# An early activation-table load, another set of dummy matmuls and a respaced K^TV stage in a two-branch linear-attention kernel

## The chip, the cores and the metric

The kernel runs on one core of a Trainium2 chip. The metric is the device time of one execution in microseconds (us); lower is better. A profile's span is a little over 1 us shorter than the time of the same execution (189.2 against 190.54 us for the kernel before). All comparisons use runs of the fast state only (a kernel has a second, slower state in some executions).

## The reference, cut to what matters

Two linear-attention branches A and B read the same `x` (2048 x 640, bf16). Each has its own weights. A gate mixes them.

```python
g = sigmoid((x * gate_w).sum(-1, keepdims=True))
# each branch: 32 heads of 20 columns
q, k, v = split(x @ wqkv)
phi = lambda t: where(t > 0, t + 1, exp(t)) + 1e-6
pq, pk = phi(q), phi(k)
kv  = einsum("bhsd,bhse->bhde", pk, v)
z   = einsum("bhsd->bhd", pk)
num = einsum("bhqd,bhde->bhqe", pq, kv)
den = einsum("bhqd,bhd->bhq", pq, z) + 1e-6
a   = (num / den) @ wo
out = g * a + (1 - g) * b
```

The kernel never forms `v`. For each branch it makes the keys `phi(K)`, then `G = phi(K)^T x`, from it `K^TV = G Wv` (masked to the heads' blocks), then `W' = K^TV Wo`, and at the end multiplies the scaled queries by `W'`.

## The kernel before

The kernel is written as operations with dependencies; a scheduler at build time gives each engine a fixed order and each result of TensorE one or two banks of PSUM, the memory that TensorE writes to. TensorE follows the order of the program text. The start: dummy matmuls ("warm"), transposes of the first two x tiles on TensorE, then key matmuls of both tiles while weights arrive one 128-row block at a time. In the profile lines XN is x as loaded, XT its transpose, WKW the key weights and `ps` any PSUM bank.

```python
def warm(n):
    for i in range(n):
        op("PE", lambda e: e.matmul(psw(bw, 512), ONE[:, :],
           ONE[:, :].unsqueeze(1).to_broadcast([128, 4, 128]), ...), 430.0, ...)
# ... (cut)
warm(6)
pss = [Buf("k", "ps", 2) for _ in range(2)]
x_tp(0)                          # five transposes of x tile 0
k_step("A", 0, 0, pss[0])        # 512 + 128 columns
x_tp(1)
k_step("A", 0, 1, pss[0])
# ... 18 further key steps of tiles 0 and 1, then for t = 2..15 both branches
```

A finished key tile is turned into phi(K) by ScalarE and VectorE; only then are its PSUM banks free for a later tile:

```python
op("ACT", ... activation(EK[...], psw(ps, D), ACT.Exp) ..., name="ke")       # L533
op("DVE", ... tensor_scalar(EK[...], EK[...], 1.0, EPS, min, add) ..., name="kt")   # L536
op("DVE", ... scalar_tensor_tensor(PKt[X][:, t, :], psw(ps, D), 0.0, EK[...], max, add) ..., name="ks")  # L544
```

Late in the kernel branch B's denominator, K^TV and W' stand between "partial outputs" of branch A (`o_part`, ten matmuls each, which fill TensorE while other engines work):

```python
o_part(0); o_part(1); o_part(2)   # one call per line in the program
den("B")                          # four 32-column matmuls; ScalarE then reads their bank
kv_unit("B")                      # two groups, 20 and 10 matmuls, each into its own bank, then a VectorE mask
o_part(3)
for u in range(NU):               # NU = 6
    wp_unit("B", u)               # two matmuls, then a ScalarE copy
    if u % 2:
        o_part(4 + u // 2)
for t in range(7, NOA):           # NOA = 12 partial outputs in all
    o_part(t)
```

Of the kernel before, what the change touches and what calls it, by code (L numbers as in the profile page):

```python
# [6 lines left out]
ACT = mybir.ActivationFunctionType  # L7
# [67 lines left out]
class Sched:  # L75
# [7 lines left out]
    def op(self, eng, fn, cost, ins=(), outs=(), after=(), prio=None, name="", dma=None):  # L83
        if eng == "ACT" and dma is None:
            after = list(after) + self.consts
        o = Op(eng, fn, cost, list(ins), list(outs), after, len(self.ops) if prio is None else prio, name, dma)
        self.ops.append(o)
        return o
# [171 lines left out]
def body(nc, A_x, A_wqkv, A_wo, B_x, B_wqkv, B_wo, gate_w, out, log=None):  # L260
# [7 lines left out]
    bf, f32 = dt.bfloat16, dt.float32  # L268
    sb = nc.alloc_sbuf_tensor
# [10 lines left out]
    PK = {X: sb("PK" + X, [128, NT * D], bf) for X in XS}  # L280
# [22 lines left out]
    GSf = GS["A"][:, :, :].rearrange("p c f -> p (c f)")  # L303
    PQ["B", 3] = GSf[:, 0:2560].rearrange("p (g s) -> p g s", g=NC)
    FXT = {"A": WV["A"][:, :, :].rearrange("p c f -> p (c f)")[:, 0:2048].rearrange("p (b s) -> p b s", b=NB), "B": XNf[:, 0:2048].rearrange("p (b s) -> p b s", b=NB)}
    NOA = 12
    OA = [XNf[:, 2048 + 1280 * i : 3328 + 1280 * i].bitcast(f32) for i in range(6)]
    OA += [PK["B"][:, 1280 * i : 1280 * i + 1280].bitcast(f32) for i in range(6)]
    NEK, NEQ, NOS = 4, 4, 4
    EK = sb("EK", [128, NEK, D], bf)  # L310
    EQ = EK[:, :, :].rearrange("p k f -> p (k f)")[:, 0 : NEQ * 512].rearrange("p (k f) -> p k f", k=NEQ)
# [12 lines left out]
    GG = sb("GG", [128, 2, NT], f32)  # L324
    GT = sb("GT", [128, 32], f32)
    ONE = sb("ONE", [128, 128], bf)
    EPSC = sb("EPSC", [128, 1], f32)
    PS = nc.alloc_psum_tensor("ps", [128, 8, 512], f32)

# [7 lines left out]
    op = sch.op  # L337

    def psw(b, w):
        return PS[:, b.slot : b.slot + b.n, :].rearrange("p a b -> p (a b)")[:, 0:w]  # L340
# [15 lines left out]
    def mm_cost(n):  # L356
        return n / 2.4 + 2.5

    def act_cost(n):
        return 190 + 0.833 * n  # L360

    def dve1(n):
        return 155 + 1.04 * n
# [5 lines left out]
    bxn = [Buf("xn%d" % t) for t in range(NT)]  # L369
    bxt = [Buf("xt%d" % t) for t in range(NT)]  # L370
    bwk = {(X, c): Buf("wk%s%d" % (X, c)) for X in XS for c in range(NC)}
    bcst, bone, beps, bgwb = Buf("cst"), Buf("one"), Buf("eps"), Buf("gwb")
    bwq = {X: Buf("wq" + X) for X in XS}
    bwv = {X: Buf("wv" + X) for X in XS}
    bwo = {X: Buf("wo" + X) for X in XS}

    op("DVE", lambda e: e.memset(ONE[:, :], 1.0), 120.0, outs=[bone], name="one")
    sch.consts = [op("POOL", lambda e: e.memset(EPSC[:, :], EPS), 100.0, outs=[beps], name="eps")]
    bxo = Buf("xo")
    op("POOL", lambda e: e.memset(XN[:, :, D : D + 1], 1.0), 200.0, outs=[bxo], name="xones")  # L380

# [45 lines left out]

    bw = Buf("warm", "ps")

    def warm(n):  # L430
        for i in range(n):
            op(
                "PE",
                lambda e: e.matmul(psw(bw, 512), ONE[:, :], ONE[:, :].unsqueeze(1).to_broadcast([128, 4, 128]), start=True, stop=True),  # L434
                430.0,
                ins=[bone],
                outs=[bw],
                name="warm",
            )

    def x_tp(t):
        for lo, hi in ((0, 1), (1, 3), (3, 5)):
            bt = Buf("tp", "ps")
            for c in range(lo, hi):
                op(
                    "PE",
                    lambda e, c=c, lo=lo, bt=bt: e.matmul(  # L447
                        PS[:, bt.slot, 128 * (c - lo) : 128 * (c - lo) + 128],
                        XN[:, t, 128 * c : 128 * c + 128],
                        IDN,  # L450
                        start=True,
                        stop=True,
                    ),
                    100.0,
                    ins=[bxn[t], bcst],
                    outs=[bt],
                    name="tp%d" % t,
                )
            half = Buf("xth")
            op(  # L460
                "DVE",
                lambda e, lo=lo, hi=hi, bt=bt: e.tensor_copy(
                    XT[:, lo:hi, 128 * t : 128 * t + 128],
                    PS[:, bt.slot, 0 : 128 * (hi - lo)].rearrange("p (c s) -> p c s", c=hi - lo),
                ),
                dve1(128 * (hi - lo)),
                ins=[bt],
                outs=[half],
                name="tpc%d" % t,
            )  # L470
            bxt[t].parts = getattr(bxt[t], "parts", []) + [half] * (hi - lo)
# [22 lines left out]
    def k_step(X, t, c, ps):  # L494
        w = D + 1 if X == "B" else D

        def fn(e):
            a = psw(ps, w)
            l = XT[:, c, 128 * t : 128 * t + 128]
            e.matmul(a[:, 0:512], l, WK[X][:, c, 0:512], start=(c == 0), stop=(c == NC - 1))  # L500
            return e.matmul(a[:, 512:w], l, WK[X][:, c, 512:w], start=(c == 0), stop=(c == NC - 1))  # L501

        xin = [bxt[t].parts[c] if hasattr(bxt[t], "parts") else bxt[t]]
        op(
            "PE",
            fn,
            mm_cost(512) + mm_cost(128),
            ins=xin + [bwk[X, c]] + ([bgc] if X == "B" else []),
            outs=[ps],
            name="k%s%d_%d" % (X, t, c),  # L510
        )
# [39 lines left out]
    def k_unit(X, t):  # L551
# [2 lines left out]
            k_step(X, t, c, ps)  # L554
        k_post(X, t, ps)

    warm(6)
    pss = [Buf("k", "ps", 2) for _ in range(2)]
    x_tp(0)
    k_step("A", 0, 0, pss[0])  # L560
    x_tp(1)
    k_step("A", 0, 1, pss[0])
    k_step("A", 1, 0, pss[1])
# [13 lines left out]
    for t in range(2, NT):  # L577
# [12 lines left out]
        ins=[bgg, bge2] + bge,  # L590
        outs=[bgg2],
        prio=LOW + 52,
        name="gm",
# [9 lines left out]
    for i, X in enumerate(XS):  # L603
        for j in range(NB):
# [8 lines left out]
                ins=bgd,  # L613
                outs=[b],
# [46 lines left out]
    def kv_unit(X):  # L661
        gv = GS[X][:, :, :].rearrange("p c (g m) -> p c g m", g=NC)
        for us in ((0, 1, 2, 3), (4, 5)):
            ps = Buf("kv", "ps")

            def fn(e, us=us, ps=ps):
                for i, u in enumerate(us):
                    lo = GR * u if u < 5 else D - GR
                    for c in range(NC):
                        r = e.matmul(  # L670
                            PS[0:GR, ps.slot, GR * i : GR * i + GR],
                            WV[X][:, c, lo : lo + GR],
                            gv[:, c, :, lo // 5 : lo // 5 + 24],
                            start=(c == 0),
                            stop=(c == NC - 1),
                        )
                return r

            op("PE", fn, 5 * len(us) * mm_cost(GR), ins=[bwv[X]] + [bgs[X, g] for g in range(NC)], outs=[ps], name="kv" + X)
            b = Buf("kvl")  # L680
            bkvl[X].append(b)
            n = len(us)
            op(
                "DVE",
                lambda e, us=us, ps=ps, n=n: e.tensor_tensor(
                    out=KVL[X][:, us[0] : us[0] + n, :].rearrange("p u (m g) -> p u g m", g=NC),
                    in0=PS[0:GR, ps.slot, 0 : GR * n].rearrange("p (u g m) -> p u g m", u=n, g=NC),
                    in1=BDM.unsqueeze(1).unsqueeze(1).to_broadcast([GR, n, NC, 24]),
                    op=ALU.mult,
                ),  # L690
                dve1(GR * n),
                ins=[ps, bcst],
                outs=[b],
                prio=-1,
                name="kvm",
            )
# [99 lines left out]
    def scale_now(X, b, h):  # L796
        pqs_op[X, b, h].prio = len(sch.ops)
# [32 lines left out]
    def den(X):  # L830
# [17 lines left out]
        for h in range(2):  # L848
# [4 lines left out]
                "ACT",  # L853
                lambda e, q=q: e.activation(DTT[:, q], PS[:, ps.slot, q], ACT.Identity, bias=EPSC[:, 0:1], scale=1.0),
                act_cost(256),
# [86 lines left out]
    def o_part(t):  # L942
        ps, b = Buf("oa", "ps", 2), Buf("oas")
        boa[t] = b
        o_mm("A", t, ps, 0, D, last="A")
        op("ACT", lambda e: e.activation(OA[t], psw(ps, D), ACT.Copy), act_cost(D), ins=[ps], outs=[b], name="oac")

    def o_rest(t):
        ps = Buf("o", "ps", 2)
        o_mm("B", t, ps, 0, D, first="B")  # L950
        o_post(t, ps, 0, D, "ADD")
# [29 lines left out]
    def out_unit(t):  # L981
        ps = Buf("o", "ps", 2)
        for X in XS:
            o_mm(X, t, ps, 0, D)
        o_post(t, ps, 0, D, "ACT")
# [52 lines left out]
    o_part(1)  # L1038
    o_part(2)
    den("B")  # L1040
    kv_unit("B")
    o_part(3)
    for u in range(NU):
        wp_unit("B", u)
        if u % 2:
            o_part(4 + u // 2)
    for t in range(7, NOA):
        o_part(t)
    for b in range(3):
        for h in range(2):  # L1050
            scale_now("B", b, h)
    for t in range(NOA):
        o_rest(t)
    for h in range(2):
        scale_now("B", 3, h)
    for t in range(NOA, NT - 1):
        out_unit(t)
# [41 lines left out]
```

## Time and profile before

| | before |
|---|---|
| time, median of the first 3 runs | 190.91 us (190.69 to 191.21) |
| span of the profile | 189.2 us |
| TensorE busy | 98% |
| first key matmul of the third tile starts | 10.75 us |
| last matmul starts | 186.85 us |

The page's busy table and its chain of waits. In the first line each engine has busy us, its share of the span and its number of instructions; the second gives shares of the span.

```profile
PE 184.9 (98%) x1245; PEld 107.8 (57%) x1269; DVE 127.3 (67%) x251; ACT 95.6 (51%) x171; POOL 0.3 (0%) x6
...
PE 96%; ACT 1%; issue 1%; DVE 1%; DVEq 0%; ACTq 0%
```

TensorE (PE) is both the busiest engine and nearly the whole chain. So a change without fewer matmuls can only close holes between them, or let more of them run at the fast rate (below). The list of waits for TensorE of the kernel before (who waited, for whom, us in total, times, longest) names few:

```profile
PE ps L434 <- DVE ONE L377: 0.4, 1, 0.4
PE ps L500 <- DVE PKA L544: 0.3, 1, 0.3
PE ps L752 <- issue: 0.2, 1, 0.2
```

A recorded matmul lasts longer than the time it blocks the next one: at full rate a 512-column matmul lasts 0.38 us but the next starts 0.216 us after it, a 128-column one 0.22 us and 0.056 us. A hole is therefore best read from start to start. The timeline shows the one in the middle line of the list (start us, us, engine, line, operation, tiles; brackets hold the idle time and its releaser):

```profile
7.48 1.28 ACT L533 ACT_TABLE_LOAD   x1 [7.48 <-PE ps L501]
...
8.77 1.30 ACT L533 ACTIVATE EK<-ps 128x640 bf16<-128x640 f32 x2
...
9.87 0.82 DVE L544 SCALAR_TENSOR_TENSOR PKA<-ps,EK 128x640 bf16<-128x640 f32 x1
...
10.23 0.22 PE L501 MATMUL ps<-WKW,XT 128*128 128x129 bf16 x1
...
10.75 0.39 PE L500 MATMUL ps<-WKW,XT 128*128 128x512 bf16 x1 [0.30 <-DVE PKA L544]
```

The table load stands in front of the first exponential; VectorE ends the tile at 9.87 + 0.82 = 10.69; the third tile's matmul follows at 10.75. From 10.23 it should have started 0.06 us later, so the hole is 0.46 us (0.47 by the unrounded starts).

The start of the same kernel on TensorE:

```profile
0.39 2.74 PE L434 MATMUL ps<-ONE 128*128 128x512 bf16 x6 [0.39 <-DVE ONE L377]
2.93 0.74 PE L447 MATMUL ps<-CST,XN 128*128 128x128 bf16 x5
3.71 0.58 PE L500 MATMUL ps<-WKW,XT 128*128 128x512 bf16 x1
4.09 0.31 PE L501 MATMUL ps<-WKW,XT 128*128 128x128 bf16 x1
4.41 0.45 PE L447 MATMUL ps<-CST,XN 128*128 128x128 bf16 x5
4.83 0.39 PE L500 MATMUL ps<-WKW,XT 128*128 128x512 bf16 x1
```

The key matmul of 512 columns lasts 0.58 us at 3.71 and 0.39 us at 4.83: between them the array goes from a slow to a fast rate. The Trainium skill describes this ("TensorE: Matmul & The Clock Gate", section "Part 1: The HAM clock gate"): a window that runs freely decides it.

The late stage, from the timeline of all engines:

```profile
143.54 0.40 PE L835 MATMUL ps<-TSH,CST 128*32 128x512 bf16 x4
...
143.87 2.02 PE L670 MATMUL ps<-GSB,WVB 128*120 128x120 bf16 x30
...
144.24 0.83 ACT L854 ACTIVATE DTT<-ps,EPSC 128x256 f32<-128x256 f32 x2
...
144.75 0.95 DVE L864 RECIPROCAL RCT<-DTT 128x128 f32<-128x128 f32 x1 [1.44 <-ACT DTT L854]
...
145.62 2.10 DVE L685 TENSOR_TENSOR KVLB<-ps,CST 120x480 bf16<-120x480 f32 x2
...
145.94 1.30 PE L922 MATMUL ps<-WPA,EX 128*128 128x128 bf16 x9
...
147.19 0.40 PE L706 MATMUL ps<-WOB,KVLB 120*120 120x512 bf16 x1
```

The order is denominator (L835), K^TV (L670), a partial output (L922), first W' (L706). A partial output has ten matmuls; the record of its first, of 512 columns, is missing here (x9), as one is about every 7 to 8 us all through this trace (1245 records). I count such a gap as 0.22 us of work.

### The profile page before, as it was taken

The numbers are of one execution on the slowest core, as the hardware profiler recorded it, in microseconds if no ns is written. First come the engines' busy times: TensorE is split into PE (matmuls) and PEld (weight loads), VectorE is DVE, ScalarE is ACT, GpSimd is POOL, SyncE is SP. The second block draws the span as 40 slices with busy tenths as digits, with TensorE's granted clock in tenths as the row PEclk, the third lists the DMA queues.
The fourth block names the chain that finished last, engine by engine and source line by source line (L and its number), as shares of the span: only waits on it lengthen the run. The fifth ranks groups of instructions, "written<-read, shape, count | busy, mean of one in ns | idle before, by whom it ended". The sixth has DMA issues, their size and how long they took to land.

```text
span 189.2 us, 3185 instructions
## 1 busy us (share of the span) xinstructions
PE 184.9 (98%) x1245; PEld 107.8 (57%) x1269; DVE 127.3 (67%) x251; ACT 95.6 (51%) x171; POOL 0.3 (0%) x6
## 2 busy tenths in 40 slices
PE   9999999999999999999999999999999999999995
PEld 3555555555565566656557556655666555555552
DVE  2299888888833546478787698888996926865300
ACT  0475655656554545545584777876624875000112
POOL 0000000000000000000000000000000000000000
DMA  7989999997024011015010005430020153233322
GB/s 208 260 169 141 198 384 369 367 222 167 6 48 101 2 37 35 0 35 31 7 27 7 3 5 142 115 93 5 1 52 16 27 167 94 73 136 108 107 69 69
DMA packets 29469, 19.42 MB, mean 103 GB/s; under 512 B 17390, under 2 KB 29198, under 8 KB 29454
## 3 DMA queue, kind: packets, MB, share of 16 engines
q1 hardware_dynamic: 29300, 19.17, 39.8%
q8 instruction: 10, 0.16, 0.4%
q10 hardware_dynamic: 154, 0.05, 0.1%
q14 instruction: 5, 0.04, 0.1%
HBM read 9.95 MB, written 2.64 MB: 67 GB/s over the span
## 4 chain that ended last, share of the span: by engine, by line
PE 96%; ACT 1%; issue 1%; DVE 1%; DVEq 0%; ACTq 0%
PE ps L922 23%; PE ps L752 22%; PE ps L629 18%; PE ps L500 17%; PE ps L630 5%; PE ps L501 5%; PE ps L670 2%; PE ps L434 1%; PE ps L706 1%; ACT L533 1%; PE ps L447 1%; DVE PKA L544 0%; ACT EK L533 0%; PE ps L707 0%; PE ps L835 0%
## 5 line engine op out<-in xcount | busy, mean ns | idle before, releaser
L500 PE MATMUL ps<-WKW,XT 128*128 128x512 bf16 x154 | 43.3, 381 | 0.4 <-DVE PKA L544 0.3
L769 ACT ACTIVATE EK<-ps 128x512 bf16<-128x512 f32 x40 | 23.9, 599 | 31.3 <-PE ps L752 30.1
L501 PE MATMUL ps<-WKW,XT 128*128 128x128 bf16 (+1 forms) x160 | 35.2, 220 | 0.3
L500 PEld LDWEIGHTS ps<-WKW,XT 128*128 128x128 bf16 x160 | 15.7, 98 | 19.6 <-DVE PKA L544 0.6
L533 ACT ACTIVATE EK<-ps 128x640 bf16<-128x640 f32 x32 | 22.3, 704 | 7.8 <-DVE EK L536 4.1
L752 PE MATMUL ps<-XT,WQA 128*128 128x512 bf16 x96 | 24.0, 379 | 0.1
L752 PE MATMUL ps<-XT,WQB 128*128 128x512 bf16 x95 | 23.3, 379 | 0.4 <-issue 0.2
L629 PE MATMUL ps<-XN,PKB 128*128 128x512 bf16 x80 | 23.5, 379 | 0.0
L779 DVE TENSOR_SCALAR EK<-EK 128x512 bf16<-128x512 bf16 x40 | 11.6, 291 | 17.5 <-ACT EK L769 17.4
L629 PE MATMUL ps<-XN,PKA 128*128 128x512 bf16 x78 | 23.1, 379 | 0.1
L630 PE MATMUL ps<-XN,PKA 128*128 128x129 bf16 x80 | 17.6, 220 | 0.1
L630 PE MATMUL ps<-XN,PKB 128*128 128x129 bf16 x80 | 17.6, 220 | 0.0
L922 PE MATMUL ps<-WPA,EX 128*128 128x128 bf16 (+1 forms) x116 | 16.8, 296 | 0.2
L922 PE MATMUL ps<-WPB,PKA 128*128 128x512 bf16 (+1 forms) x118 | 16.4, 298 | 0.1
L752 PEld LDWEIGHTS ps<-XT,WQB 128*128 128x128 bf16 x100 | 10.9, 118 | 8.5 <-issue 0.2
L501 PEld LDWEIGHTS ps<-WKW,XT 128*128 128x128 bf16 x160 | 15.7, 98 | 0.0
L536 DVE TENSOR_SCALAR EK<-EK 128x640 bf16<-128x640 bf16 x32 | 10.4, 325 | 7.7 <-ACT EK L533 7.7
L752 PEld LDWEIGHTS ps<-XT,WQA 128*128 128x128 bf16 x100 | 10.7, 117 | 8.1
L968 ACT ACTIVATE TSB<-ps 128x640 bf16<-128x640 f32 (+1 forms) x4 | 2.7, 677 | 23.9 <-PE ps L922 23.9
L629 PEld LDWEIGHTS ps<-XN,PKA 128*128 128x128 bf16 x80 | 9.4, 117 | 7.9
L629 PEld LDWEIGHTS ps<-XN,PKB 128*128 128x128 bf16 x80 | 9.4, 117 | 7.8
L544 DVE SCALAR_TENSOR_TENSOR PKB<-ps,EK 128x640 bf16<-128x640 f32 x16 | 13.2, 825 | 0.6
(77 smaller groups left out, 231.1 us busy)
## 6 DMA issues: line engine op xcount, KB each, us to landing
out_dram<-TSB SPq DMA_DIRECT2D x15, 160.0 KB, 1.8
XN<-in_A_x_dram SPq DMA_DIRECT2D x1, 2240.0 KB, 9.3
WKW<-in_A_wqkv_dram SPq DMA_DIRECT2D x5, 160.0 KB, 3.4
WKW<-in_B_wqkv_dram SPq DMA_DIRECT2D x5, 160.0 KB, 4.2
WQA<-in_A_wqkv_dram SPq DMA_DIRECT2D x1, 800.0 KB, 11.0
WQB<-in_B_wqkv_dram SPq DMA_DIRECT2D x1, 800.0 KB, 13.4
WVA<-in_A_wqkv_dram SPq DMA_DIRECT2D x1, 800.0 KB, 12.8
WVB<-in_B_wqkv_dram SPq DMA_DIRECT2D x1, 800.0 KB, 13.9
```

Source lines behind the costliest of these rows:

```text
L500: e.matmul(a[:, 0:512], l, WK[X][:, c, 0:512], start=(c == 0), stop=(c == NC - 1))
L501: return e.matmul(a[:, 512:w], l, WK[X][:, c, 512:w], start=(c == 0), stop=(c == NC - 1))
L533: op("ACT", lambda e: e.activation(EK[:, ek.slot, :], psw(ps, D), ACT.Exp), act_cost(D), ins=[ps] + first, outs=[ek], name="ke")
L536: lambda e: e.tensor_scalar(EK[:, ek.slot, :], EK[:, ek.slot, :], 1.0, EPS, op0=ALU.min, op1=ALU.add),
L544: lambda e: e.scalar_tensor_tensor(PKt[X][:, t, :], psw(ps, D), 0.0, EK[:, ek.slot, :], op0=ALU.max, op1=ALU.add),
L629: e.matmul(a[:, 0:512], l, XN[:, t, 0:512], start=(t == 0), stop=(t == NT - 1))
L630: return e.matmul(a[:, 512 : D + 1], l, XN[:, t, 512 : D + 1], start=(t == 0), stop=(t == NT - 1))
L670: r = e.matmul(PS[0:GR, ps.slot, GR * i : GR * i + GR], WV[X][:, c, lo : lo + GR], gv[:, c, :, lo // 5 : lo // 5 + 24], start=(c == 0), st ...
L752: r = e.matmul(PS[:, ps.slot, :], WQ[X][:, c, g::5], XT[:, c, 512 * b : 512 * b + 512], start=(c == 0), stop=(c == NC - 1),)
L769: lambda e: e.activation(EQ[:, eq.slot, :], PS[:, ps.slot, :], ACT.Exp),
L779: lambda e: e.tensor_scalar(EQ[:, eq.slot, :], EQ[:, eq.slot, :], 1.0, EPS, op0=ALU.min, op1=ALU.add),
L922: r = e.matmul(a[:, l0 - lo : h0 - lo], PQ[X, b][:, g, 128 * (t % 4) : 128 * (t % 4) + 128], WP[X][:, g, l0:h0], start=(X == first and g = ...
```

## The change

Three parts: load the activation table at once by a dummy exponential; five dummy matmuls instead of six ahead, and two small ones after the first key step, to keep TensorE busy while the second x tile arrives; in branch B one more partial output in front of K^TV, the W' units spread one and two between partial outputs, and 13 partial outputs instead of 12. The diff, cut of buffer names:

```diff
-    NOA = 12
+    NOA = 13
@@
-    OA += [PK["B"][:, 1280 * i : 1280 * i + 1280].bitcast(f32) for i in range(6)]
+    OA += [PK["B"][:, 1280 * i : 1280 * i + 1280].bitcast(f32) for i in range(7)]
@@
+    SCR = sb("SCR", [128, 1], f32)
@@
+    op("ACT", lambda e: e.activation(SCR[:, :], EPSC[:, :], ACT.Exp), 1500.0, ins=[beps], outs=[bge0], prio=10**6, name="table")
@@
-    def warm(n):
+    def warm(n, w=4):          # w * 128 columns (body cut)
@@
-    warm(6)
+    warm(5)
     pss = [Buf("k", "ps", 2) for _ in range(2)]
     x_tp(0)
     k_step("A", 0, 0, pss[0])
+    warm(2, 1)
     x_tp(1)
@@
     den("B")
+    o_part(3)
     kv_unit("B")
-    o_part(3)
+    o_part(4)
     for u in range(NU):
         wp_unit("B", u)
-        if u % 2:
-            o_part(4 + u // 2)
-    for t in range(7, NOA):
+        if u % 2 == 0:
+            o_part(5 + u // 2)
+    for t in range(8, NOA):
         o_part(t)
```

More of the change, by code (lines that the diff above doesn't have):

```diff
@@ L371, in body @@
     bwk = {(X, c): Buf("wk%s%d" % (X, c)) for X in XS for c in range(NC)}
-    bcst, bone, beps, bgwb = Buf("cst"), Buf("one"), Buf("eps"), Buf("gwb")
+    bcst, bone, beps, bge0 = Buf("cst"), Buf("one"), Buf("eps"), Buf("ge0")
     bwq = {X: Buf("wq" + X) for X in XS}
@@ L433, in warm @@
                 "PE",
-                lambda e: e.matmul(psw(bw, 512), ONE[:, :], ONE[:, :].unsqueeze(1).to_broadcast([128, 4, 128]), start=True, stop=True),
-                430.0,
+                lambda e: e.matmul(psw(bw, 128 * w), ONE[:, :], ONE[:, :].unsqueeze(1).to_broadcast([128, w, 128]), start=True, stop=True),
+                107.0 * w,
                 ins=[bone],
```

## The prediction

> **What bounds the kernel now.** The busy table gives TensorE 98% of the 189.2 us span, and the chain of waits is TensorE for 96%. The list of waits shows three for TensorE: 0.4 us for the first memset, 0.3 us for VectorE (key stage, L544), 0.2 us of "issue". From 10.8 to 187 us matmuls follow each other almost without holes; only holes can be saved.
>
> **1. Early table load (the real gain).** In the timeline ScalarE loads its table for 1.28 us at 7.48 us, when the first key tile is complete; its exponential starts at 8.77, VectorE finishes the tile at about 10.7, and TensorE, which needs those PSUM banks, stops: a matmul of about 0.06 us starts at 10.23, the next at 10.75. A hole of 0.46 us. The Trainium skill ("ScalarE: Activation LUTs", section "What ACT_TABLE_LOAD costs") gives about 1283 ns for the load; the trace agrees with 1.283 us. With the dummy exponential the load sits at roughly 1.2 to 2.5 us, behind ScalarE's two DMA issues, where ScalarE is idle. The first tile is then free at about 9.45, before TensorE asks for it (10.29); the transposed x for the next tile landed at 10.05. So the hole should go whole, but no more: 0.46 of the 1.28 us.
>
> **2. Five dummies ahead, two small behind.** Cold 512-column dummies start 0.43 us apart, so one fewer could let the transposes start at about 2.6 instead of 2.93 (x and the constants had landed by 2.5). But the second x tile lands at 4.37, the second key weights at 4.79, and the last of these limits is B's second weight tile at 8.05, used at 8.10. The 0.3 us is given back to these DMAs. The small dummies (estimate: 2 x 0.11 us) fall into the wait before 4.37. Worth 0 to 0.05 us. Clock: matmuls go from the slow to the fast rate at about 4.05. The Trainium skill ("TensorE: Matmul & The Clock Gate", "The HAM clock gate") ties this to a free-running window of about 3.4 us. I expect the switch still near 4 us; slipping a whole window would lose 1 to 2 us.
>
> **3. K^TV and W' of branch two spread, a 13th partial output.** Same matmuls in another order. Holes there now: about 0.09 us before the denominator (it waits for the VectorE sums, unchanged), 0.10 us behind it, 0.11 us before the first W' (VectorE mask). The last goes, perhaps part of the second: 0.1 to 0.15 us. The extra VectorE add has slack. The tail (last matmul at 186.85, end at 189.2) is unchanged.
>
> **Sum:** 0.46 + 0.03 + 0.1, about 0.6 us of 190.91: 190.35 us. Range 190.0 to 190.8; the three runs of before spread over 0.5 us. Faster by over 2%: 0.01; within 2%: 0.98; slower by over 2%: 0.01.
>
> **Right if** the table load shows before 3 us with the first key exponential at about 7.5; the list of waits loses TensorE's wait for L544; the matmul at 8.1 still waits for B's second weight DMA; the start of the third tile's key matmuls moves from 10.75 to about 10.3; TensorE is unbroken from there, and the first W' has no hole.
>
> **Wrong if** a different PSUM bank assignment (the dummies now hold a bank through the first transposes) makes an early unit wait, the clock switches later, or weight DMAs land later in the new runs; or if the third tile's transposed x lands later than 10.3, which would cap the gain of step 1.

## The result, and the profile after

| | before | changed |
|---|---|---|
| median of 6 runs | 190.80 us (190.48 to 191.42) | 190.24 us (189.91 to 190.51) |
| ratio, 95% interval | | 0.9966 (0.9944 to 0.9987) |
| profiled run / its span | 190.54 / 189.2 us | 190.32 / 189.0 us |
| third tile's first matmul | 10.75 us | 10.89 us |
| last matmul | 186.85 us | 186.63 us |

Ratios are the mean time of one kernel's fast runs over that of the other's of the same rounds, so not quite the ratio of the medians quoted. The verdict is "same" at 2%, and the time lies in the predicted range. But the profile does not agree with the way there: the third tile starts 0.14 us later, not 0.45 us earlier, and the gain is made up after it. Page and waits of the changed kernel:

```profile
PE 184.9 (98%) x1246; PEld 108.3 (57%) x1270; DVE 128.6 (68%) x252; ACT 95.9 (51%) x172; POOL 0.3 (0%) x6
...
PE 96%; DMA 2%; issue 1%; SPq 0%; DVE 0%; DVEq 0%
```

```profile
PE ps L436 <- DVE ONE L378: 0.4, 1, 0.4
PE ps L755 <- issue: 0.2, 1, 0.2
```

The wait for the key stage's VectorE instruction has left the list. The timeline shows why; its lines answer to those of before:

```profile
1.18 1.28 ACT L380 ACT_TABLE_LOAD   x1 [1.18 <-issue]
...
8.09 1.30 ACT L535 ACTIVATE EK<-ps 128x640 bf16<-128x640 f32 x2 [5.42 <-PE ps L503]
...
9.19 0.82 DVE L546 SCALAR_TENSOR_TENSOR PKA<-ps,EK 128x640 bf16<-128x640 f32 x1
...
10.83 0.22 PE L503 MATMUL ps<-WKW,XT 128*128 128x129 bf16 x1
10.89 0.38 PE L502 MATMUL ps<-WKW,XT 128*128 128x512 bf16 x1
```

The load is out of the way, VectorE ends the first tile at 9.19 + 0.82 = 10.01 us, and the hole is gone: 0.06 us from 10.83 to 10.89. Yet TensorE itself arrives 0.60 us later than before (10.83 against 10.23). The start on TensorE shows where that comes from:

```profile
0.39 2.31 PE L436 MATMUL ps<-ONE 128*128 128x512 bf16 x5 [0.39 <-DVE ONE L378]
2.72 0.69 PE L449 MATMUL ps<-CST,XN 128*128 128x128 bf16 x5
3.46 0.59 PE L502 MATMUL ps<-WKW,XT 128*128 128x512 bf16 x1
...
3.95 0.42 PE L436 MATMUL ps<-ONE 128*128 128x128 bf16 x2
4.51 0.72 PE L449 MATMUL ps<-CST,XN 128*128 128x128 bf16 x5
5.02 0.63 PE L502 MATMUL ps<-WKW,XT 128*128 128x512 bf16 x1
...
6.05 0.38 PE L502 MATMUL ps<-WKW,XT 128*128 128x512 bf16 x1
```

In this run the rate rises only at 6.0 us: the 512-column matmul at 5.02 still lasts 0.63 us. The late stage on TensorE, with one more partial output between denominator (L838) and K^TV (L673):

```profile
143.66 0.40 PE L838 MATMUL ps<-TSH,CST 128*32 128x512 bf16 x4
144.00 1.53 PE L925 MATMUL ps<-WPA,EX 128*128 128x512 bf16 x10
145.37 1.81 PE L673 MATMUL ps<-GSB,WVB 128*120 128x120 bf16 x30
147.23 1.31 PE L925 MATMUL ps<-WPA,EX 128*128 128x128 bf16 x9
148.37 0.38 PE L709 MATMUL ps<-WOB,KVLB 120*120 120x512 bf16 x1
```

From the start of K^TV to that of the group behind it: 145.94 - 143.87 = 2.07 us before, 147.23 - 145.37 = 1.86 us after, each with one missing record. From there to the first W': 1.25 us before, 1.14 us after. These are 0.21 and 0.11 us of closed holes. From the third tile's first matmul to the last matmul of the kernel the time is 186.85 - 10.75 = 176.10 us before and 175.74 us after (unrounded starts): 0.36 us, more than twice what was predicted for this part.

So there were three questions: is the hole in front of the third tile really worth 0.46 us, what in the third part gives 0.36 us, and does the changed start cause the late rate switch or did chance?

### The profile page after: what moved, and what is told of

It is laid out like the page before. It is cut to its first block, busy times and chain, and to the rows that moved or that the text cites. A ratio compares the mean times of both kernels' runs of the same rounds, so it can differ in the third digit from the quotient of the medians.

```text
span 189.0 us, 3188 instructions
## 1 busy us (share of the span) xinstructions
PE 184.9 (98%) x1246; PEld 108.3 (57%) x1270; DVE 128.6 (68%) x252; ACT 95.9 (51%) x172; POOL 0.3 (0%) x6
## 4 chain that ended last, share of the span: by engine, by line
PE 96%; DMA 2%; issue 1%; SPq 0%; DVE 0%; DVEq 0%
PE ps L925 23%; PE ps L755 22%; PE ps L632 18%; PE ps L502 18%; PE ps L503 5%; PE ps L633 5%; DMA XN<-in_A_x_dram 2%; PE ps L673 2%; PE ps L709 1%; SPq L349 0%; PE ps L449 0%; PE ps L710 0%; PE ps L838 0%; DVE TSB L969 0%; PE ps L483 0%
## 5 line engine op out<-in xcount | busy, mean ns | idle before, releaser
L925 PE MATMUL ps<-WPB,PKA 128*128 128x128 bf16 (+1 forms) x117 | 16.1, 297 | 0.2
L971 ACT ACTIVATE TSB<-ps 128x640 bf16<-128x640 f32 (+1 forms) x3 | 2.0, 668 | 23.2 <-PE ps L925 23.2
L546 DVE SCALAR_TENSOR_TENSOR PKA<-ps,EK 128x640 bf16<-128x640 f32 x16 | 13.2, 825 | 0.6
```

The source lines that it names most:

```text
L546: lambda e: e.scalar_tensor_tensor(PKt[X][:, t, :], psw(ps, D), 0.0, EK[:, ek.slot, :], op0=ALU.max, op1=ALU.add),
L925: r = e.matmul(a[:, l0 - lo : h0 - lo], PQ[X, b][:, g, 128 * (t % 4) : 128 * (t % 4) + 128], WP[X][:, g, l0:h0], start=(X == first and g = ...
```

## The experiments

Twelve runs were made: ten new kernels, one of them (dummies_only) twice, and the changed kernel again. All gave correct results. One table holds what their profiles show, so that the start and the rest can be told apart. "Switch" is when the matmuls' rate rises (from the spacing of their starts and their durations; each value is of one profile); "hole" is the extra spacing in front of the third tile's first matmul; "rest" is from that matmul's start to the last matmul's.

| kernel | switch, us | third tile, us | hole, us | rest, us | ratio to before (95%) |
|---|---|---|---|---|---|
| before | 4.1 to 4.4 | 10.75 | 0.47 | 176.10 | 1 |
| changed | 6.0 | 10.89 | 0 | 175.74 | 0.9966 (0.9944 to 0.9987) |
| changed_again | 5.9 | 10.79 | 0 | 175.74 | 0.9961 (0.9946 to 0.9975) |
| table_only | 3.1 | 10.38 | 0 | 176.09 | 0.9974 (0.9962 to 0.9986) |
| dummies_only | 3.2 to 3.5 | 10.69 | 0.53 | 176.10 | 1.0016 (1.0000 to 1.0032) |
| dummies_again | 6.4 | 11.70 | 0.53 | 176.11 | 1.0024 (0.9987 to 1.0060) |
| spread_only | 3.8 | 10.76 | 0.53 | 175.75 | 0.9981 (0.9969 to 0.9994) |
| kv_later | 5.4 | 10.96 | 0.53 | 175.75 | 0.9974 (0.9959 to 0.9988) |
| six_dummies | 3.3 | 10.63 | 0 | 175.74 | 0.9958 (0.9942 to 0.9974) |
| filled | 3.5 | 10.52 | 0 | 175.74 | 0.9946 (0.9931 to 0.9960) |
| filled_den_late | 5.2 | 10.54 | 0 | 175.75 | 0.9937 (0.9922 to 0.9953) |
| no_dummies | 7.5 to 7.6 | 11.65 | 0 | 175.74 | 1.0003 (0.9985 to 1.0020) |
| act_delay_short | 3.6 | 10.15 | 0 | 175.74 | 0.9948 (0.9927 to 0.9970) |
| act_delay_long | 3.2 to 3.5 | 11.22 | 0.67 | (slow) | 0.9999 (0.9977 to 1.0021) |

### changed_again: the changed kernel a second time

No edit.

> The changed kernel unaltered, a second sample. Theory: 0.5 to 0.8 us below the kernel before in the mean (0.46 + 0.34 + 0 from the dummies, less what chance does to the clock). If the late clock switch at 6.0 us is chance, this profile may show another time for it; if the changed start causes it, it is near 6.0 us again.

Measured: median 189.93 us (189.71 to 190.55), ratio 0.9961, which is 0.74 us. The switch came at 5.9 us in this profile, near the 6.0 us of the first. That speaks for the rival that the changed start causes it; dummies_only below, with the same start, contradicts it.

### table_only: part one alone

Edit on the kernel before:

```diff
+    SCR = sb("SCR", [128, 1], f32)
@@
+    bge0 = Buf("ge0")
+    op("ACT", lambda e: e.activation(SCR[:, :], EPSC[:, :], ACT.Exp), 1500.0, ins=[beps], outs=[bge0], prio=10**6, name="table")
```

> Part one alone: the kernel before plus the dummy exponential. Theory (the hole of 0.46 us at 10.3 us is the whole worth of the early table load): about 0.46 us below the kernel before in the mean; in the trace the table load before 3 us, and no hole between the last of the first twenty key matmul pairs and the third tile's. Rival (a late clock switch hides the hole, as the changed kernel's profile with its switch at 6.0 us suggests): nearer 0.2 us.

Measured: median 190.25 us, ratio 0.9974, which is 0.50 us of 190.76 (0.27 to 0.72 by the interval). TensorE at the third tile in its timeline:

```profile
10.32 0.22 PE L504 MATMUL ps<-WKW,XT 128*128 128x129 bf16 x1
10.38 0.38 PE L503 MATMUL ps<-WKW,XT 128*128 128x512 bf16 x1
```

The hole is gone, and with an early switch the third tile starts at 10.38 us, as predicted for the whole change. The theory stands; the rival's 0.2 us lies outside the interval. What follows the third tile is unchanged (176.09 us).

### act_delay_short and act_delay_long: how much of ScalarE's time counts there

Edit on the changed kernel; one or three extra exponentials in front of the first key exponential, their result unused (the line that allocates SCD is cut):

```diff
+        if X == "A" and t == 0:
+            for _ in range(1):          # 3 in the long one
+                late = Buf("late")
+                op("ACT", lambda e: e.activation(SCD[:, :], psw(ps, 352), ACT.Exp), act_cost(352), ins=[ps] + first, outs=[late], name="late")
+                first = [late]
         op("ACT", ... name="ke")
```

> The changed kernel with one extra exponential of 352 columns (about 0.5 us of ScalarE) in front of the first key exponential. Theory (the table load's first 0.8 us were slack, only its rest was a hole): no hole in TensorE in front of the third tile, time of the changed kernel within the scatter of the clock switch. Rival (every us on ScalarE counts there): +0.5 us, and a hole of that size.

> The same with three such exponentials (about 1.45 us of ScalarE, a little over the 1.28 us table load). Theory: a hole of 0.5 to 0.7 us comes back in front of the third tile, released by VectorE, and the time rises by that over the changed kernel. Rival: none, or the full 1.45 us.

Measured: the short delay (0.46 us in the trace) left no hole and a median of 189.71 us; the long one brought the hole back, and its three fast runs had 190.54, 190.83 and 191.28 us. The two ratios differ by 0.51%, about 1 us, and their intervals do not overlap. That is more than the hole alone; in so few runs the scatter of the rate switch may be the rest, which is not shown. The profile of the long one fell in the slow state (its matmuls are some 3% further apart), so only the waiting relation is read from it:

```profile
7.66 1.46 ACT L539 ACTIVATE SCD<-ps 128x352 bf16<-128x352 f32 x3 [4.98 <-PE ps L504]
...
11.22 0.38 PE L503 MATMUL ps<-WKW,XT 128*128 128x512 bf16 x1 [0.49 <-DVE PKA L552]
```

So ScalarE has slack there of between 0.46 us, which left no hole, and the 1.28 us of the table load, which left one. An estimate from the kernel before: 1.28 us of load gave 0.46 us of hole, so about 0.8 us was slack.

### spread_only and kv_later: which part of the late stage pays

spread_only is the last hunk of the change with `NOA` and `OA`, on the kernel before. kv_later keeps 12 partial outputs and the W' units in pairs, and only moves K^TV behind one partial output, with another between it and the first W':

```diff
     den("B")
+    o_part(3)
     kv_unit("B")
-    o_part(3)
+    o_part(4)
     for u in range(NU):
         wp_unit("B", u)
         if u % 2:
-            o_part(4 + u // 2)
-    for t in range(7, NOA):
+            o_part(5 + u // 2)
+    for t in range(8, NOA):
```

> Part three alone: K^TV one partial output later, W' spread, 13 partial outputs. As predicted: 0.10 to 0.15 us gained. By the two traces: 0.34 us, because K^TV's own holes go as well (0.22 us inside and at its start) with the 0.15 us around the first W'. In the trace TensorE should have no hole over 0.05 us between the denominator and the last W'.

> Kernel before with K^TV one partial output later and W' still in pairs, one partial output in front of each pair (12 partial outputs). Theory: the second K^TV group no longer waits for ScalarE to read the denominator's bank; the holes at and in K^TV (0.22 us together) go, and so does that of 0.11 us before the first W', because the mask is done during the partial output as before but with a shorter VectorE queue: 0.3 us gained, most of spread_only's. Rival (the W' respacing does it): under 0.1 us.

Measured: spread_only 190.52 us, ratio 0.9981 (-0.36 us; 0.11 to 0.59 by the interval); kv_later 190.34 us, ratio 0.9974, not distinguishable from it by time. The traces are sharper: both have a rest of 175.75 us against 176.10. kv_later on TensorE:

```profile
145.44 1.81 PE L670 MATMUL ps<-GSB,WVB 128*120 128x120 bf16 x30
147.09 1.52 PE L922 MATMUL ps<-WPA,EX 128*128 128x512 bf16 x10
148.45 0.38 PE L706 MATMUL ps<-WOB,KVLB 120*120 120x512 bf16 x1
```

Here no record is missing: K^TV takes 147.09 - 145.44 = 1.65 us, the partial output behind it 1.36 us, which is ten matmuls at full rate. The position of K^TV gives the whole 0.36 us; the respacing of the W' units and the thirteenth partial output give nothing beyond it. From the third tile to the denominator the traces of before and kv_later take the same 132.78 us, so all of it lies behind the denominator.

Where was it lost before? In the program as it is built from the kernel before, the second K^TV group writes the denominator's PSUM bank, and its first matmul waits for the semaphore that ScalarE raises after its two reads of that bank. The trace agrees: those reads (L854 in the last fence of the profile before) end at 144.24 + 0.83 = 145.07 us, and K^TV's 21st matmul, after the 20 of the first group, starts at 145.13 us. Two narrow windows of the timeline (`--engine PE --window 145.121:145.129` and `145.2:145.22`) show the 20th and the 21st:

```profile
144.96 0.22 PE L670 MATMUL ps<-GSB,WVB 128*120 128x120 bf16 x1
...
145.13 0.26 PE L670 MATMUL ps<-GSB,WVB 128*120 128x120 bf16 x1
```

They start 0.17 us apart where the others of the group are 0.055 us apart, so about 0.12 us are lost. Another 0.05 us precedes the second matmul of each group, and 0.11 us the first W', whose mask on VectorE (L685, from 145.62) stood behind the denominator's reciprocal (L864, to 145.70). Some 0.04 us more are two spacings of the first W' pair that are 0.02 us too long each. With one partial output in front of K^TV, the bank has long been read. Nothing separates the bank from the other waits by experiment; what is shown is that moving K^TV closes them all.

### dummies_only, twice: part two alone

Edit: only the `warm` lines of the change.

> Part two alone: five large dummies ahead and two small behind. Theory: no gain in the mean, within 0.15 us of the kernel before; the transposes start about 0.2 us earlier, but the second tile's still wait for the second x tile near 4.4 us. Rival (the dummies change when the clock rises): a mean shift of 0.3 us or more either way, and a switch near 6 us in this profile too.

> dummies_only once more, for the sign of part two: +0.31 us with an interval from 0.0 to 0.6 in the first sample. If fewer dummies really delay the clock switch more often, again 0.2 us or more above the kernel before; if the first sample was chance of the switch, within 0.15 us of it.

Measured: 190.47, 191.42, 191.28, 190.99, 191.27 and 191.15 us (+0.31 us; 0.00 to 0.61), then 190.73 to 191.48 us and one run of 193.22 us that was still counted as fast (+0.46 us; -0.25 to +1.14). Neither interval allows a gain of more than 0.25 us, and neither excludes zero. In the profile of the first sample the switch came early and the third tile stood at 10.69 us, no better than before: the transposes start at 2.75 us, but the second x tile's wait until 4.20 us. In that of the second the switch came at 6.4 us, and the third tile stood at 11.70 us. One kernel, two profiles, switches some 3 us apart.

### six_dummies, filled, no_dummies: is the late switch caused or met?

six_dummies is the changed kernel with the old start. filled has six large dummies, two small ones between the first transposes and the first key step, and three behind it. no_dummies has none.

```diff
# filled, on the changed kernel
-    warm(5)
+    warm(6)
     pss = [Buf("k", "ps", 2) for _ in range(2)]
     x_tp(0)
+    warm(2, 1)
     k_step("A", 0, 0, pss[0])
-    warm(2, 1)
+    warm(3, 1)
     x_tp(1)
# six_dummies: warm(6) and no warm(2, 1);  no_dummies: neither
```

> The changed kernel with its start put back: six large dummies, no small ones. Parts one and three alone measured -0.50 and -0.36 us by the ratios, so 0.8 to 0.9 us below the kernel before if the dummies' change is worth nothing or costs. Theory now (the changed start makes the array less busy in its first microseconds, and the clock rises late more often): runs lie closer together, switch before 4.5 us in the profile, mean 0.1 us or more below the changed kernel's -0.74 us. Rival (late switches are chance of phase alone): same as the changed kernel, -0.65 to -0.75 us, and the same scatter of about 0.8 us.

> Six large dummies ahead and the two waits of the first tile filled with small ones (two between the transposes and the first key step, three behind it). Theory: array busy almost without holes up to 4.5 us, so the switch is early in all runs, as good as six_dummies within 0.15 us or better, scatter small. Rival (phase alone): same scatter as the changed kernel.

> The changed kernel without any dummy matmul. Theory: the array begins only with the transposes near 2.7 us and idles between, the switch comes at 6 us or later in every run, and the mean is 0.3 to 1.0 us above the changed kernel. Rival (the window does not care for the first 2.5 us): no change over 0.15 us.

Measured, in the order above: 190.10 us (189.64 to 190.46), 189.94 us (189.64 to 189.95, five runs), 191.10 us (190.59 to 191.28). Without dummies the rate rises only between 7.5 and 7.6 us, in the one profile taken:

```profile
7.05 0.61 PE L502 MATMUL ps<-WKW,XT 128*128 128x512 bf16 x1
7.45 0.28 PE L503 MATMUL ps<-WKW,XT 128*128 128x128 bf16 x1
7.56 0.39 PE L502 MATMUL ps<-WKW,XT 128*128 128x512 bf16 x1
```

Its third tile starts at 11.65 us against 10.79 to 10.89 us, and by the ratios it loses 0.7 to 0.8 us against the changed kernel (intervals that do not overlap for the second sample, and just touch for the first) and 0.9 us against six_dummies of the same rounds. So the dummies as such are worth 0.7 to 0.9 us. Whether six or five plus two of them is better stays open: six_dummies against the changed kernel is 0.9958 against 0.9961 and 0.9966, and its scatter of 0.8 us is no smaller. The expected narrower scatter did not come. The switch came late in three of six profiles with the changed start (6.0, 5.9, 6.4 us), and in one of five with the old one (5.4 us in kv_later). filled's five runs lie within 0.31 us, but filled_den_late, with the same start, had a switch at 5.2 us. With these counts chance is enough.

### filled_den_late: the hole in front of the denominator

Edit on filled: everything from the denominator of branch B on comes one partial output later.

> filled, with the denominator of branch two (and all behind it) one partial output later. If the hole of 0.09 us in front of the denominator is a wait for VectorE's sums, as the prediction said, it goes and the kernel is 0.09 us below filled; if it belongs to the denominator's matmuls themselves (branch one's denominator shows the same 0.09 us though nothing is waited for), it stays, and the time is filled's within 0.1 us.

Measured: 189.76 us (189.42 to 189.96), and a rest of 175.75 us against filled's 175.74. The timeline of the stage:

```profile
142.32 0.75 DVE L819 SCALAR_TENSOR_TENSOR TSH<-GSA,ZC,TSB 128x512 bf16<-128x512 bf16 x1
...
144.66 0.10 PEld L839 LDWEIGHTS ps<-TSH,CST 128*32 128x32 bf16 x4 [0.26 <-issue]
```

The last VectorE sum ends at 143.07 us, 1.6 us before the denominator, and the weight load waits for nothing but issue. Still 0.09 us of extra spacing stand in front of the four matmuls. So this hole belongs to them, not to VectorE.

This kernel has the lowest ratio of all, 0.9937. Its interval overlaps those of the changed kernel (upper end 0.9953 against lower ends 0.9944 and 0.9946), and they ran in other rounds, so it may not be called better than the changed kernel; better than the kernel before it is.

## Why the prediction was right or wrong, point by point

The total was right: 190.35 us predicted, 190.24 us measured. It was right partly by luck, because two errors lean against each other: in its profiles the start gained less than predicted (the third tile stood later than before), the late stage more.

- *Step 1, "0.46 of the 1.28 us"*: right. table_only measured 0.50 us by time, and in its trace the hole is gone and the third tile is at 10.38 us. Delays of 0.46 and 1.46 us on ScalarE show the slack and the hole separately (the hole in a slow profile). The Trainium skill's figure for the load ("ScalarE: Activation LUTs", section "What ACT_TABLE_LOAD costs", about 1283 ns) agreed with the 1.28 us of both traces.
- *"The start of the third tile's key matmuls moves from 10.75 to about 10.3"*: failed in the changed kernel's own profiles (10.89 and 10.79 us). The hole had gone, but TensorE arrived late because the rate rose at 6.0 and 5.9 us. For the same reason the first key exponential was at 8.09 us instead of 7.5, and the matmul that was to wait for B's second weight block did not wait: the block landed at 7.83 us, before TensorE needed it. The prediction had named a later clock switch among its reasons to be wrong.
- *Step 2, "Worth 0 to 0.05 us"*: not settled. Part two alone measured +0.31 and +0.46 us with intervals that touch zero; a loss is more likely than a gain, but it may be chance. The mechanism predicted for its early side was right: starting the transposes earlier is given back to the second x tile.
- *"I expect the switch still near 4 us"*: the failed step. It took one profile's value, read as 4.05 us, for a property of the kernel. Over the profiles with dummies it came between 3.1 and 6.4 us, and twice for one kernel at 3.2 to 3.5 and at 6.4 us. The skill's free-running window would have allowed to foresee that; the prediction quoted it, with about 3.4 us, and still took one value. The 3.3 us between the earliest and the latest switch are about the length of such a window, as chance would give; no run tests that. Its "1 to 2 us" for a late switch was about 1.0 us where it can be seen, between the third tiles of dummies_only (10.69 us) and dummies_again (11.70 us); other waits of these two starts are not taken out.
- *Step 3, "0.1 to 0.15 us"*: the mechanism (holes around K^TV and the first W') was right, the term was mis-sized: 0.36 us. The prediction counted 0.11 us in front of the first W', which went, and part of the 0.10 us behind the denominator, of which nothing went (0.32 us from the denominator to the next matmul in both kernels). It left out the holes inside K^TV (0.12 us in front of its second group, twice 0.05 us), which are not in the list of waits for TensorE.
- *"About 0.09 us before the denominator (it waits for the VectorE sums)"*: wrong cause, right in effect. It is there with the sums ready 1.6 us earlier.

The sum of the single parts by time, 0.50 + 0.36 less 0.31 or 0.46, is 0.4 to 0.55 us; the whole measured 0.65 and 0.74 us by the ratios. The intervals allow that. six_dummies, which is parts one and three together, measured 0.80 us by its ratio against 0.50 + 0.36 = 0.86 us, so these two add up.

## What to carry to other kernels

In a kernel that is bound by one engine, add up start-to-start spacing against the full-rate spacing, stage by stage: it shows small waits (a bank still being read, a mask not yet done) that a list of waits leaves out, and it compares two traces to 0.01 us where timed runs scatter by 0.8 us. Put a unit of independent work between a producer and both its bank's next user and its consumer. Load the activation table where the engine is idle anyway, but count only what the slack does not cover; and judge the first 10 us of a kernel from several profiles, since the moment when the array reaches its full rate changes from run to run.

## What the Trainium skill lacked or had wrong

- "TensorE: Matmul & The Clock Gate", "Part 1: The HAM clock gate", puts the transition "around 4µs into sustained matmul activity, ±500ns run-to-run". The first dummy is at 0.39 us. Where no hole over 0.26 us stood before the switch, it came 2.7 us (table_only) to 5.0 us (kv_later) after that; with the larger holes of the changed start as much as 6.0 us (dummies_again). A later note on the same page says that the count of cold matmuls is run-variable, which agrees.
- The same section does not say how full the window has to be. Here a hole of 0.25 us between the transposes and the first key matmul did not hinder a switch at 3.2 to 3.5 us (dummies_only), while without dummies it came between 7.5 and 7.6 us.
- "ScalarE: Activation LUTs", "What ACT_TABLE_LOAD costs", adds a drain of about 1380 ns to the load "for every switch to a different set". The first load of this kernel, on an idle engine, shows none behind it: the load starts at 7.48 us, lasts 1.28 us, and the exponential starts at 8.77 us.
- "TensorEngine Tiling (Array Packing)", "Key Properties", says that changing the tiling mode drains TensorE, but gives no time for it. Here 0.09 us of extra spacing stand in front of the denominator's four 32-column matmuls and 0.10 us behind them, in every trace. That the drain is their cause is not shown.
